# Attention products with V: which are issued in halves, and behind which group of scores

## The chip, the cores and the metric

The kernel runs on one core of a Trainium2 chip. The metric is the time of one execution on the device, in microseconds (us). A core has five engines that this text speaks of: PE (TensorE, matrix products; its weight loads are shown apart as PEld), DVE (VectorE), ACT (ScalarE), POOL (GpSimd) and SP (SyncE, which here only issues transfers). Each works through its own instructions in order and waits for the others by semaphores.

## The reference

Two attention blocks over 2048 tokens with 512 channels and 32 heads of 16 are mixed by a gate. A attends causally inside segments of 512 tokens and adds a compressive memory; B attends over all 2048 tokens.

```python
g = _sigmoid((x * gate_w).sum(-1, keepdims=True))
# A, for each of four segments s:
logits = einsum("bhqd,bhkd->bhqk", qs, ks) * scale + mask      # 512 x 512, causal
a_dot = einsum("bhqk,bhkd->bhqd", softmax(logits), vs)
o = gm * num / den + (1 - gm) * a_dot                          # gm = sigmoid(beta); num, den from M, z
M = M + einsum("bhld,bhle->bhde", phi(ks), vs)
# B:
p = softmax(einsum("bhqd,bhkd->bhqk", q, k) * Dh ** -0.5)      # 2048 x 2048
out = g * (concat(o) @ A_wo) + (1 - g) * (einsum("bhqk,bhkd->bhqd", p, v) @ B_wo)
```

## The kernel before

**Units and slots.** A unit is four heads by 512 queries. There are 32 units of A and 32 of B, and after a first phase (projections, the memory, all keys and values to DRAM and back) the kernel runs 32 slots; slot k computes unit k of A and unit 32+k of B. A unit of B has 16 blocks of 128 keys, one of A has four blocks of its own segment, of which the causal mask leaves 512, 384, 256 and 128 query columns.

**Groups.** A slot is a loop over 37 groups (`NG`). Groups 0 to 31 belong to B: group n takes block n//2 and one pair of its four heads. Groups 32 to 36 belong to A (`GA`, packed so that each fills two banks of 512 columns: block 0 in groups 32 and 33, blocks 1 and 3 together in 34 and 35, block 2 in 36). In each group, in this order:

- `t_group` writes the transposed scores of two heads to two banks of PSUM (L502, two matmuls, side by side on halves of the array) and has ACT turn each bank into exponentials in the buffer `raw` (L508). Three banks are used in turn (`T3`: two `tb` and `mb`), so the second bank of a group is the first bank of the group before, and is free only when ACT has read it. For A, POOL then zeroes the masked corner of what ACT wrote (L511).
- The tasks of `plan`: as a rule one piece of the plain scores of a later unit, `s_b` (L448) or in groups 32 to 36 and 0 `s_a` (L427, L430), whose maximum DVE takes (L450, L434, L436). These go to two double banks, `sbk`.
- In group 20 of the slots from 9 on, one half of an output projection, `out_mm` (L590, twelve matmuls into one of the three banks); its result is copied by ACT (even halves, L594) or added by DVE (odd halves, L597).
- `pvs(k, n)`: products of the exponentials with V, by `pv` (L524). For each of the four heads a matmul of 17 columns of weights (16 of V and one of ones, which gives the softmax's sum) accumulates in a strip of 32 partitions of one bank, `pvb`; the trace shows two records for each such matmul.

**The products before.** For B, block b's product is issued in two halves of 256 query columns, the first in group 2b+2 and the second in group 2b+3; so each group from 2 to 33 holds one half, and block 15 falls into groups 32 and 33, beside A's first scores. After the second half of block 15 `fin_copy` (L533, ACT) takes the bank `pvb` to `pvs` and stores it. Then follow A's products into the same bank: block 0 in two halves in groups 34 and 35, blocks 1 and 3 in group 36, block 2 in group 0 of the next slot, with its `fin_copy` (L531, DVE). Group 1 has no product. Slot 31 issues B's blocks whole, in odd groups, and has two banks more for its scores.

Behind group 21 of a slot stands `m_chain` (L459 to L469, four small operations of DVE on the maxima), and its result is spread into the queries by `m_rows` in group 24. `fin_load`, `fin_rec`, `fin_bc` and `fin_norm` carry the stored sums and outputs of a unit through division and gate; they lie beside the groups on SP, DVE and POOL.

Of the kernel before, what the change touches and what calls it, by code (L numbers as in the profile page):

```python
# [23 lines left out]
NT = SEQ // 128  # L24
# [5 lines left out]
OMI = 10  # L30
# [3 lines left out]
def gated_mix_kernel(ctx, tc, x, wq, wk, wv, wo, beta, wqkv, wob, gate_w, out):  # L34
# [479 lines left out]
    def pv(u, it, lo=0, hi=None):  # L514

        kd, qd, c = UN[u]
        g, q = divmod(qd, 2)
        q0 = 128 * it if kd == "A" else 0
        hi = hi or C - q0
        last = 2 if kd == "A" else NT - 1  # L520
        vt = VA[(u // 2) % 2] if kd == "A" else VB[g % 2]
        for h in range(4):
            pt = PT[u, it, h]
            nc.tensor.matmul(PVB[32 * h:32 * h + E + 1, q0 + lo:q0 + hi], vt[:, it, 4 * q + h, :], pt[:, lo:hi],  # L524
                             start=it == 0 and lo == 0, stop=it == last and q0 + hi == C, skip_group_check=True)

    def fin_copy(u):

        ps = W.tile([128, C], FT, name="pvs", bufs=1)
        if u < 31:  # L530
            nc.vector.tensor_copy(ps, PVB)  # L531
        else:
            nc.scalar.activation(ps, PVB, AF.Copy)  # L533
        AT["pd", u] = D.tile([4, 32, C], FT, name=f"pd{u}")
        nc.sync.dma_start(AT["pd", u].rearrange("h r t -> (h r) t"), ps)
# [36 lines left out]
    def load_wo(g):  # L572
        for a, w in enumerate((wo, wob)):
            raw = AT["o"][1][:, g, a]
            nc.sync.dma_start(raw, w[g * 128:(g + 1) * 128, :])
            nc.gpsimd.tensor_copy(AT["wh"][:, g, a], raw)
            nc.gpsimd.tensor_tensor(AT["wl"][:, g, a], raw, AT["wh"][:, g, a], op=OP.subtract)
# [142 lines left out]
    for blk in range(16):  # L720
# [12 lines left out]
        n = blk + 1 + (c == 2)  # L733
# [92 lines left out]
    def pvs(k, n):  # L826

        ua, ub = k, 32 + k
        if n == 0:
            if k:  # L830
                pv(ua - 1, 2)
                fin_copy(ua - 1)
        elif k == 31 and n < 2 * NT:
            if n % 2 and n > 1:
                pv(ub, n // 2 - 1)
        elif 2 <= n < 2 * NT + 2:
            pv(ub, n // 2 - 1, n % 2 * 256, n % 2 * 256 + 256)
            if n == 2 * NT + 1:
                fin_copy(ub)
        elif n > 2 * NT + 1:  # L840
            m = n - 2 * NT - 2
            if m < 2:
                pv(ua, 0, 256 * m, 256 * m + 256)
            else:
                pv(ua, 1)
                pv(ua, 3)

    def extras(k):

# [55 lines left out]
    for k in range(32):  # L905
        ua, ub = k, 32 + k
        banks = T3 + [SBK[0][:, n] for n in range(2)] * (k == 31)
        for n in range(NG):
            it = n // 2 if n < NG - 1 else NT + 2
            t_group(*(ub, n) if n < 2 * NT else (ua, n - 2 * NT), banks)  # L910
            for f in plan.get((k, n), []) + ex[k][0].get(n, []):
                f()
            pvs(k, n)
            for f in ex[k][1].get(n, []):
                f()
# [19 lines left out]
            if it == 9:  # L935
                if k % 2 == 0 and k < 30:
                    load_vb(k // 2 + 1)
                if 1 <= k <= 4:
                    load_wo(k - 1)
    pv(31, 2)  # L940
    fin_copy(31)
    fin_bc(63)
    den = AT["d"][0][64:]
# [51 lines left out]
```

## Time and profile before

| what | value |
|---|---|
| three timed runs | 2005.86, 2013.76, 2010.57 us (median 2010.57) |
| the profiled execution's own time | 2007.75 us |
| its span in the profile | 2006.0 us, granted clock 0.995 |
| one slot, 1 to 8 (between the DVE copies L531) | 47.96 to 48.71 us |
| one slot, 9 to 29 | 50.89 to 52.54 us |
| DVE, ACT, POOL busy, share of the span | 81%, 72%, 13% |

A row of the timeline gives the start and the length in us, engine, line, operation, what it writes and reads, the shapes, how many instructions are merged in it, and in brackets how long the engine was idle before and what ended that. A row of waits gives the engine and line that waited, for whom, the total in us, how often, and the longest. A PE record contains the filling and emptying of the array, so two records in a row overlap; how long a matmul holds PE is read from start to start.

### The profile page before, as it was taken

The numbers are of one execution on the slowest core, as the hardware profiler recorded it, in microseconds if no ns is written. First come the engines' busy times: TensorE is split into PE (matmuls) and PEld (weight loads), VectorE is DVE, ScalarE is ACT, GpSimd is POOL, SyncE is SP. The second block draws the span as 40 slices with busy tenths as digits, with TensorE's granted clock in tenths as the row PEclk, the third lists the DMA queues.
The fourth block names the chain that finished last, engine by engine and source line by source line (L and its number), as shares of the span: only waits on it lengthen the run. The fifth ranks groups of instructions, "written<-read, shape, count | busy, mean of one in ns | idle before, by whom it ended". The sixth has DMA issues, their size and how long they took to land.

```text
span 2006.0 us, 43688 instructions
## 1 busy us (share of the span) xinstructions
PE 1956.3 (98%) x17517; PEld 949.0 (47%) x17517; DVE 1631.9 (81%) x1825; ACT 1435.1 (72%) x2703; POOL 256.6 (13%) x474
## 2 busy tenths in 40 slices
PE   8999999999999999999999999999999999999988
PEld 7777777444444344444444444444444444444434
DVE  6135665799999999999999999999899999899832
ACT  3233332688888888888787888787878787878883
POOL 2200000011110101111111111111111111111111
PEclk9999999999999999999999999999999999999999
DMA  7765656644443445343435344444444545444101
GB/s 222 164 190 177 197 180 177 148 106 112 95 112 85 104 93 109 81 110 81 109 79 112 85 112 85 112 85 112 85 112 85 112 85 111 85 112 85 50 26 54
DMA packets 162743, 222.49 MB, mean 111 GB/s; under 512 B 39261, under 2 KB 89453, under 8 KB 156781
## 3 DMA queue, kind: packets, MB, share of 16 engines
q1 hardware_dynamic: 159596, 211.70, 43.9%
q0 software_dynamic: 2944, 8.00, 2.2%
q8 instruction: 138, 2.26, 0.5%
q14 instruction: 65, 0.52, 0.1%
HBM read 148.21 MB, written 68.16 MB: 108 GB/s over the span
## 4 chain that ended last, share of the span: by engine, by line
PE 89%; DMA 3%; DVE 3%; ACT 2%; SPq 2%; issue 1%; POOL 0%; ACTq 0%; POOLq 0%; DVEq 0%
PE pvb L524 31%; PE tb L502 17%; PE sbk L448 12%; PE mb L502 8%; PE tb L279 3%; PE sbk L427 2%; PE tb L590 2%; PE mb L279 2%; ACT raw L508 2%; PE pvb L279 2%; DVE mxb L450 2%; PE sbk L430 2%; PE mb L590 1%; PE sbk L279 1%; PE tb L262 1%
## 5 line engine op out<-in xcount | busy, mean ns | idle before, releaser
L450 DVE TENSOR_REDUCE mxb<-sbk 128x2 f32<-128x1024 f32 x1024 | 1222.7, 1222 | 49.4 <-PE sbk L448 45.7
L508 ACT ACTIVATE raw<-tb 128x512 f32<-128x512 f32 x1557 | 886.0, 596 | 172.8 <-PE tb L502 85.6
L524 PE MATMUL pvb<-raw,vb 128*17 128x256 f32 (+1 forms) x8072 | 639.5, 389 | 0.0
L508 ACT ACTIVATE raw<-mb 128x512 f32<-128x512 f32 x780 | 465.2, 596 | 81.6 <-PE tb L502 57.5
L502 PE MATMUL tb<-qb,xh 64*128 64x512 f32 x880 | 330.9, 494 | 3.7 <-ACT raw L508 3.7
L524 PEld LDWEIGHTS pvb<-raw,vb 128*17 128x17 f32 x8072 | 133.8, 95 | 344.8 <-issue 338.4
L448 PE MATMUL sbk<-xh,qb 64*128 64x512 f32 x1344 | 287.6, 400 | 4.4 <-DVE mxb L450 3.3
L511 POOL TENSOR_SCALAR_AFFINE_SELECT raw<-raw 128x256 f32<-128x256 f32 (+1 forms) x320 | 115.4, 361 | 879.9 <-ACT raw L508 871.9
L502 PE MATMUL mb<-qb,xh 64*128 64x512 f32 x437 | 215.6, 493 | 2.0 <-ACT raw L508 2.0
L502 PEld LDWEIGHTS tb<-qb,xh 64*128 64x128 f32 x880 | 124.7, 183 | 190.5 <-issue 98.3
L502 PE MATMUL tb<-qb,kb 64*128 64x512 f32 x463 | 176.0, 496 | 4.8 <-ACT raw L508 2.8
L434 DVE TENSOR_REDUCE mx<-sbk 128x2 f32<-128x768 f32 (+1 forms) x128 | 139.8, 1092 | 43.9 <-PE sbk L430 36.2
L448 PE MATMUL sbk<-kb,qb 64*128 64x512 f32 x704 | 152.9, 408 | 0.8 <-DVE mxb L450 0.7
L448 PEld LDWEIGHTS sbk<-xh,qb 64*128 64x128 f32 x1344 | 138.8, 186 | 10.8 <-DVE mxb L450 7.0
L502 PEld LDWEIGHTS mb<-qb,xh 64*128 64x128 f32 x437 | 79.9, 183 | 89.5 <-issue 49.1
L502 PE MATMUL mb<-qb,kb 64*128 64x512 f32 x241 | 118.4, 491 | 0.8 <-DVE st L289 0.8
L502 PEld LDWEIGHTS tb<-qb,kb 64*128 64x128 f32 x463 | 65.8, 183 | 102.3 <-issue 51.4
L524 PE MATMUL pvb<-raw,va 128*17 128x256 f32 (+2 forms) x1280 | 94.7, 383 | 4.2 <-ACT pvs L533 0.8
L564 POOL TENSOR_TENSOR o<-o,d 128x512 f32<-128x512 f32 x31 | 39.7, 1282 | 415.2 <-DMA qa<-dA 177.0
L427 PE MATMUL sbk<-ka,qa 64*128 64x256 f32 (+3 forms) x512 | 86.6, 346 | 0.0
L502 PE MATMUL tb<-qa,ka 64*128 64x384 f32 (+3 forms) x340 | 79.5, 372 | 0.0
L448 PEld LDWEIGHTS sbk<-kb,qb 64*128 64x128 f32 x704 | 72.1, 185 | 12.6 <-issue 6.5
(265 smaller groups left out, 1804.5 us busy)
## 6 DMA issues: line engine op xcount, KB each, us to landing
xh<-dB SPq DMA_DIRECT2D x38, 512.0 KB
vb<-vdB SPq DMA_DIRECT2D x16, 1088.0 KB
dB<-st SPq DMA_DIRECT2D x64, 256.0 KB
dA<-st SPq DMA_DIRECT2D x64, 256.0 KB
pd<-pvs SPq DMA_DIRECT2D x64, 256.0 KB
kb<-dB SPq DMA_DIRECT2D x22, 512.0 KB
xh<-dB SPq DMA_DIRECT2D x38, 256.0 KB
qb<-dB SPq DMA_DIRECT2D x64, 128.0 KB
```

The source lines that it names most:

```text
L279: nc.tensor.matmul(b, WS[ws][w][wi][:, k, :], (XH, XL)[xi][c][:, k, :], start=n == 0, stop=n == 11)
L427: nc.tensor.matmul(b[:, j, c0:c0 + n], q_of(u)[r, p, i * 128:(i + 1) * 128], k_of(u, p)[r, :n], start=True, stop=False)
L430: nc.tensor.matmul(b[:, j, c0 + n - 128:c0 + n], crows[r, n2 - 1], cmask[r, n2 - 1], start=False, stop=n2 == 2)
L434: nc.vector.tensor_reduce(m[:, :, p, i], b[:, :, :n], axis=AX.X, op=OP.max)
L448: nc.tensor.matmul(b[:, j], q_of(u)[r, p, i * 128:(i + 1) * 128], k_of(u, p)[r, kc * C:(kc + 1) * C], start=True, stop=True)
L450: nc.vector.tensor_reduce(MXB[u][:, :, p, i, kc], b, axis=AX.X, op=OP.max)
L502: nc.tensor.matmul(bs[j][:, c0:c0 + w], k_of(u, h // 2)[r, 128 * it:128 * it + 128], q_of(u)[r, h // 2, q0:], start=True, stop=True)
L508: nc.scalar.activation(pt, bs[j], AF.Exp, scale=SCALE)
L511: nc.gpsimd.affine_select(out=m, in_=m, pattern=[[1, 128]] if n < 2 else [[0, 2], [1, 128]], compare_op=OP.is_ge, fill=0.0, base=0, channe ...
L524: nc.tensor.matmul(PVB[32 * h:32 * h + E + 1, q0 + lo:q0 + hi], vt[:, it, 4 * q + h, :], pt[:, lo:hi], start=it == 0 and lo == 0, stop=it ...
L564: nc.gpsimd.tensor_tensor(o, o, d, op=OP.mult)
L590: nc.tensor.matmul(b, (AT["oh"], AT["ol"])[oi][:, g, a], (AT["wh"], AT["wl"])[wi][:, g, a], start=n == 0, stop=n == 11)
```

## The change

Only the table of products in `pvs` and its remainder behind the loop change.

- B's block 15 is issued whole (512 columns) in group 32, and `fin_copy` of B's unit follows there; group 33 has no product.
- A's block 0 is issued whole in group 34; group 35 and group 36 have no product.
- A's blocks 1 and 3 move from group 36 to group 0 of the next slot, ahead of block 2, whose place stays. Behind the last slot the three follow the loop.
- In slots 9 to 30, B's block 9 is issued whole in group 20, behind `out_mm`; group 21 has no product.
- All other products of B stay as they were.

```diff
         if n == 0:
             if k:
-                pv(ua - 1, 2)
+                for it in (1, 3, 2):
+                    pv(ua - 1, it)
                 fin_copy(ua - 1)
-        elif k == 31 and n < 2 * NT:
+        elif n == 2 * NT:
+            pv(ub, NT - 1)
+            fin_copy(ub)
+        elif n > 2 * NT:
+            if n == 2 * NT + 2:
+                pv(ua, 0)
+        elif k == 31:
             if n % 2 and n > 1:
                 pv(ub, n // 2 - 1)
-        elif 2 <= n < 2 * NT + 2:
+        elif k >= 9 and n // 2 == OMI:
+            if n % 2 == 0:
+                pv(ub, n // 2 - 1)
+        elif n > 1:
             pv(ub, n // 2 - 1, n % 2 * 256, n % 2 * 256 + 256)
-            if n == 2 * NT + 1:
-                fin_copy(ub)
-        elif n > 2 * NT + 1:
-            m = n - 2 * NT - 2
-            if m < 2:
-                pv(ua, 0, 256 * m, 256 * m + 256)
-            else:
-                pv(ua, 1)
-                pv(ua, 3)
...
-    pv(31, 2)
+    for it in (1, 3, 2):
+        pv(31, it)
     fin_copy(31)
```

PE at the end of a slot's B part (here slot 0), groups 32 and 33: `vb` is B's V, `qa` and `ka` are A's queries and keys, and the L502 rows are the transposed scores of groups 33 and 34.

```order
 L430 MATMUL sbk_113<-cmask,crows 128x128
-L524 MATMUL pvb<-raw_86,vb_75 17x256 x4
+L524 MATMUL pvb<-raw_86,vb_75 17x512 x4
 L502 MATMUL mb<-qa_73,ka_71 128x512
 L502 MATMUL tb_109<-qa_73,ka_71 128x512
@@ -608,5 +608,4 @@
 L430 LDWEIGHTS crows
 L430 MATMUL sbk_114<-cmask,crows 128x128
-L524 MATMUL pvb<-raw_86,vb_75 17x256 x4
 L502 MATMUL tb_110<-qa_73,ka_71 128x384
 L502 MATMUL mb<-qa_73,ka_71 128x384
```

Both halves now stand ahead of group 33's scores, and group 34's scores follow group 33's with only the plain scores and their mask between them.

ACT at the same place: L508 are the exponentials of groups 32 and 33, L533 is the copy of B's finished bank.

```order
 L508 ACTIVATE raw_86<-tb_109 128x512
 L508 ACTIVATE raw_86<-tb_110 128x512
-L508 ACTIVATE raw_86<-mb 128x512
-L508 ACTIVATE raw_86<-tb_109 128x512
-L533 ACTIVATE pvs<-pvb 128x512
+L533 ACTIVATE pvs<-pvb 128x512
+L508 ACTIVATE raw_86<-mb 128x512
+L508 ACTIVATE raw_86<-tb_109 128x512
```

The copy now stands ahead of group 33's two exponentials, which wait behind it for the end of the whole product.

PE behind the projection of slot 9, before: L590 is the projection's end, L524 are B's products, L502 the scores of groups 21 and 22, L448 plain scores.

```order
L590 MATMUL tb_110<-wh,ol 128x512 x4
L524 MATMUL pvb<-raw_86,vb_75 17x256 x4
L502 MATMUL mb<-qb_70,kb_89 128x512
L502 MATMUL tb_109<-qb_70,kb_89 128x512
L448 MATMUL sbk_114<-xh_88,qb_69 128x512 x2
L524 MATMUL pvb<-raw_86,vb_75 17x256 x4
L502 MATMUL tb_110<-qb_70,kb_89 128x512
```

The same place in the changed kernel:

```order
L590 MATMUL tb_110<-wh,ol 128x512 x4
L524 MATMUL pvb<-raw_86,vb_75 17x512 x4
L502 MATMUL mb<-qb_70,kb_89 128x512
L502 MATMUL tb_109<-qb_70,kb_89 128x512
L448 MATMUL sbk_114<-xh_88,qb_69 128x512 x2
L502 MATMUL tb_110<-qb_70,kb_89 128x512
L502 MATMUL mb<-qb_70,kb_89 128x512
```

The first product has 512 columns and the second is gone, so the scores of group 22 stand right behind the plain scores of group 21.

## The prediction

> **What bounds the kernel now.** I began with the page's head and its busy shares.
>
> ```profile
> span 2006.0 us, 43688 instructions
> PE 1956.3 (98%) x17517; PEld 949.0 (47%) x17517; DVE 1631.9 (81%) x1825; ACT 1435.1 (72%) x2703; POOL 256.6 (13%) x474
> ```
>
> PE looks full, so whatever shortens PE's work should help. But an overlapping record hides a wait between two matmuls, so I read the one kind of group that already has no product, group 1 of a slot (here of slot 20), on the timeline.
>
> ```profile
> 1364.09 0.49 PE L502 MATMUL mb<-qb,xh 64*128 64x512 f32 x1
> 1364.09 0.49 PE L502 MATMUL tb<-qb,xh 64*128 64x512 f32 x1
> 1364.42 0.40 PE L448 MATMUL sbk<-kb,qb 64*128 64x512 f32 x2
> ...
> 1364.65 0.39 PE L502 MATMUL tb<-qb,xh 64*128 64x512 f32 x1
> 1364.68 0.60 ACT L508 ACTIVATE raw<-mb 128x512 f32<-128x512 f32 x1 [0.38 <-PE tb L502]
> ...
> 1365.33 0.49 PE L502 MATMUL mb<-qb,xh 64*128 64x512 f32 x1 [0.29 <-ACT raw L508]
> ...
> 1365.99 0.63 PE L524 MATMUL pvb<-raw,vb 128*17 128x256 f32 x8
> ...
> 1366.54 0.50 PE L502 MATMUL tb<-qb,xh 64*128 64x512 f32 x2
> ```
>
> Group 1's scores start at 1364.09, and PE is through its plain scores 0.56 us later: the first matmul of group 2 starts at 1364.65. The second needs the bank `mb` that ACT is reading, whose exponential ends at 1365.28, and starts at 1365.33. So **a group without a product takes 1.24 us**, and the next, with half a product, takes 1365.33 to 1366.54 = 1.21 us. The product fits into the time that a bank needs to go round: 0.53 to 0.59 from a score's start to its exponential's, 0.60 for that, 0.03 to 0.05 to the next matmul, together 1.16 to 1.24. PE's own time with half a product is about the same, so in an ordinary group both bind at once, and a half taken out of a group frees nothing.
>
> DVE is no bound in between:
>
> ```profile
> 1343.45 3.48 DVE L450 TENSOR_REDUCE mxb<-sbk 128x2 f32<-128x1024 f32 x3
> ```
>
> Back to back, three maxima take 3.48, so they start every (3.48 - 1.22) / 2 = 1.13 us, against 1.21 to 1.24 of a group.
>
> **What a product costs PE.** Half a product and the projection's surroundings (slot 19):
>
> ```profile
> 1339.32 1.07 PE L590 MATMUL mb<-wh,ol 128*128 128x512 f32 x4
> 1340.32 0.63 PE L524 MATMUL pvb<-raw,vb 128*17 128x256 f32 x8
> ...
> 1340.87 0.50 PE L502 MATMUL tb<-qb,xh 64*128 64x512 f32 x2
> 1341.21 0.40 PE L448 MATMUL sbk<-kb,qb 64*128 64x512 f32 x2
> 1341.40 1.09 ACT L508 ACTIVATE raw<-tb 128x512 f32<-128x512 f32 x2 [0.39 <-PE tb L502]
> 1341.54 0.63 PE L524 MATMUL pvb<-raw,vb 128*17 128x256 f32 x8
> ...
> 1342.10 0.49 PE L502 MATMUL tb<-qb,xh 64*128 64x512 f32 x1
> ```
>
> A whole one, in slot 31:
>
> ```profile
> 1965.76 1.05 PE L524 MATMUL pvb<-raw,vb 128*17 128x512 f32 x8
> ...
> 1966.74 0.50 PE L502 MATMUL tb<-qb,xh 64*128 64x512 f32 x2
> ```
>
> From start to start a half holds PE 1340.87 - 1340.32 = 0.55 us and a whole 0.98: a merge costs its first group 0.43 and saves 2 x 0.55 - 0.98 = 0.12 of PE in sum. The saving can only be had if the group that lost its half gets shorter by 0.55.
>
> **Edit 1: block 9 whole behind the projection** (slots 9 to 30, 22 of them). PE goes straight from L590 to the product; ACT and DVE have run dry. Group 21's scores start at 1340.87 + 0.43 = 1341.30. Before, group 22's second matmul came 1342.10 - 1340.87 = 1.23 later. Now PE could be there after 0.34 + 0.33 = 0.67 (the steps to L448 and to L524 above), but the bank is busy: group 21's exponential starts 0.53 after its scores (1341.40), takes 0.60 and releases 0.03 to 0.05 later, 1.16 to 1.18. So group 22 is late by 0.43 - 0.06 = **0.37**; bounds 0.30 (the half could gain as much as 0.13) and 0.44 (the 1.24 of group 1). Later groups carry a half again and cannot make it up. Sum 22 x 0.37 = 8.1, between 6.6 and 9.7.
>
> **Edit 2: the end of a slot** (31 places, from slot 0's group 32 to slot 30's, with group 0 of the next). Slot 19:
>
> ```profile
> 1354.76 0.49 PE L502 MATMUL mb<-qa,ka 64*128 64x512 f32 x1
> ...
> 1355.65 0.63 PE L524 MATMUL pvb<-raw,vb 128*17 128x256 f32 x8
> ...
> 1356.20 0.49 PE L502 MATMUL tb<-qa,ka 64*128 64x512 f32 x1
> ...
> 1356.79 0.60 ACT L508 ACTIVATE raw<-tb 128x512 f32<-128x512 f32 x1 [0.42 <-PE mb L502]
> 1356.99 0.62 PE L524 MATMUL pvb<-raw,vb 128*17 128x256 f32 x8
> ...
> 1357.55 0.50 PE L502 MATMUL tb<-qa,ka 64*128 64x384 f32 x4
> 1357.76 0.60 ACT L533 ACTIVATE pvs<-pvb 128x512 f32<-128x512 f32 x1
> ...
> 1358.01 0.29 POOL L511 TENSOR_SCALAR_AFFINE_SELECT raw<-raw 128x128 f32<-128x128 f32 x1 [0.20 <-ACT raw L508]
> ...
> 1358.48 0.16 PEld L524 LDWEIGHTS pvb<-raw,va 128*17 128x17 f32 x8 [0.26 <-POOL raw L511]
> ...
> 1359.07 0.44 PE L502 MATMUL tb<-qa,ka 64*128 64x384 f32 x1
> ...
> 1359.67 0.60 ACT L508 ACTIVATE raw<-mb 128x512 f32<-128x512 f32 x1 [0.32 <-PE tb L502]
> 1359.86 0.63 PE L524 MATMUL pvb<-raw,va 128*17 128x256 f32 x8
> ...
> 1360.42 0.38 PE L502 MATMUL tb<-qa,ka 64*128 64x256 f32 x1
> ...
> 1361.69 1.06 PE L524 MATMUL pvb<-raw,va 128*17 128x384 f32 x16
> ...
> 1362.68 0.49 PE L502 MATMUL tb<-qb,xh 64*128 64x512 f32 x2
> ...
> 1363.53 0.63 PE L524 MATMUL pvb<-raw,va 128*17 128x256 f32 x8
> ```
>
> From group 32 to group 1 of the next slot it takes 1364.09 - 1354.76 = 9.33 us: 1.44, 1.35, 1.52, 1.35, 2.26 and 1.41. Then:
> - *Group 32* has the whole: 1.44 + 0.43 = 1.87.
> - *Group 33* has none. PE alone would need 0.79 (1356.20 to 1356.99). But ACT now has L533 ahead of its exponentials, and L533 waits for the whole product: its start 1355.65, its record 1.05 and 0.1 to ACT give 1356.80; one ACT operation later (0.48) the exponential starts at 1357.28 instead of the 1357.15 that its scores, now at 1356.63, would allow. With 0.60 and 0.03 group 34's second matmul starts at 1357.91: 1.28 for the group.
> - *Group 34* has A's block 0 whole, which needs POOL's select on group 33's second exponential; POOL's last started 1358.01 and PE 0.47 later. The exponential comes 0.49 behind the first, so now at 1357.77, which is 0.48 later than before (0.50 behind the 1356.79 above), and the product at 1358.48 + 0.48 = 1358.96. With 0.98 the next scores start at 1359.94, so 2.03.
> - *Group 35* has none. PE alone: 0.79. The bank: 0.60 to the exponential (1359.07 to 1359.67), 0.60 and 0.03: 1.23.
> - *Group 36* has none: 1361.69 - 1360.42 = 1.27 of scores and plain scores, after which group 0 follows at once; its bank is free after 1.23 and does not hold it.
> - *Group 0*: 0.85 to the product (1362.68 to 1363.53), then the two moved ones, 1362.68 - 1361.69 = 0.99, and block 2's 0.56: 2.40. POOL has long finished.
>
> Sum 1.87 + 1.28 + 2.03 + 1.23 + 1.27 + 2.40 = 10.08, **0.75** more. The bounds: if neither L533 nor POOL costs anything (1.16 and 0.79 + 0.98 = 1.77 for groups 33 and 34, 1.16 and 1.20 for 35 and 36) it is 9.56, or +0.23; if groups 33, 35 and 36 gain nothing at all (1.35, 1.35 and 1.36) it is 10.36, or +1.03. I take the value by the rows. Sum 31 x 0.75 = 23.3, between 7.1 and 31.9.
>
> Queued behind the added waits: L531 waits on DVE for the later end of block 2, and the maxima behind it start at about group 1's plain scores anyway; the stores of `pvs` leave SP about 0.7 later and are read many groups on. The moved operations issue no other transfers.
>
> **The tail.** Slot 31 has two more banks and whole products already; there block 15's copy comes earlier, A's products later. One row for the first:
>
> ```profile
> 1971.93 0.60 ACT L533 ACTIVATE pvs<-pvb 128x512 f32<-128x512 f32 x1
> ```
>
> By the rule of group 32 it starts some 0.9 earlier, and PE's last products some 0.6 later; I count 0, within 1 us either way.
>
> **Sum.** 2007.75 + 8.1 + 23.3 = 2039.2 us on the profiled execution's own time, which is 2.8 under the median shown; so **2039**. Bounds 2007.75 + 13.7 = 2021 and 2007.75 + 41.6 = 2049.
>
> **Rivals.**
>
> *PE's work decides (faster).* Block 15 and block 0 in 32 slots and block 9 in 22 are 86 merges at 0.12, or 10.3 us less: 1997. It holds if a group without product ends with PE's own 0.67 to 0.79, that is if the bank's round were shorter than that. For it: 98% busy. The Trainium skill (Perfetto Trace Analysis, Engine Utilization) says that in a well-optimized kernel at least one engine should approach full utilization, which read for PE gives this rival. Against it: 0.29 of idle ahead of L502 in a group that has no product. The Trainium skill (TensorE: Matmul & The Clock Gate, Wait — 56ns, not 53.3ns?) puts the fixed cost of one more back-to-back matmul at about 2.5 ns; eight records fewer in a merge would be 0.02 us, an estimate from that page, and this rival would then be worth 1.7 us; the rows above show 0.12, and they decide. 0.07.
>
> *The end of the slot comes out even.* Before, ACT stands still behind group 36 while blocks 1 and 3 run:
>
> ```profile
> 1363.21 1.09 ACT L508 ACTIVATE raw<-tb 128x512 f32<-128x512 f32 x2 [1.11 <-PE tb L502]
> ```
>
> The change starts these exponentials earlier. Were 0.75 of the 0.99 hidden under them, edit 1 alone would remain: 2016. Against it: group 0 holds only 1.1 of ACT's work and would be 2.40 long, so ACT stands still there instead. 0.08.
>
> *DVE collides.* Group 24's plain scores wait for the maximum behind `m_chain`.
>
> ```profile
> PE sbk L448 <- DVE mxb L450: 3.9, 6, 1.3
> ```
>
> Edit 1 shifts that maximum 0.43 and the scores only 0.37, so such waits can become more; at 1.3 in each of the eleven even slots from 10 to 30 they would add 14: 2053. 0.07.
>
> **How the numbers follow.** The forecast has 0.78. Its own range is 2021 to 2049; with the spread of the runs (5 below to 3 above their median) and part of the third rival I give **2020 to 2052**. A measurement of this kernel can tell about 0.5%, 10 us, from no change. Faster by more: the first rival, 0.07. Within: the second, 0.08, and little else. Slower: 0.85.
>
> **What would show it.** Right: in groups 33, 35 and 21, PE's rows L502 idle before ACT's L508, as only group 1 shows it now; groups 32 to 1 add up to about 10.1; slots 1 to 8 take 48.7, the later ones 52.0; DVE's and ACT's busy time is unchanged. Wrong: if group 33 or 21 is shorter than 1.1, the bank does not bind and the first rival holds; if group 0 to 1 is well under 2.4, the moved products are hidden; if the loss is there but L448 waits for DVE, it is the third.

## The result and the profile after

The changed kernel takes 2058.53 us (median of 6 runs, 2056.88 to 2065.93) against 2008.07 before (median of 6): a ratio of 1.0252, with a 95% interval of 1.023 to 1.0273. It is slower, as forecast, but by 50 us instead of 31, and outside the range.

The page's head of the changed kernel:

```profile
span 2059.8 us, 42280 instructions
PE 1971.4 (96%) x16829; PEld 961.3 (47%) x16829; DVE 1635.3 (79%) x1825; ACT 1432.7 (70%) x2703; POOL 256.4 (12%) x474
```

The busy times of ACT, DVE and POOL are as before: the 50 us are waiting. PE's row shows that only in part: its busy time grew by 15 us, although its products take less of it.

From start to start of DVE's copy L531, a slot of 1 to 8 took 47.99 us before (median) and 49.34 now, an odd slot from 9 on 50.92 and 52.69. So a slot's end costs 1.35, and the projection's group another 0.4. 31 x 1.35 + 22 x 0.4 = 51, about the whole difference. (An even slot from 10 on grew by less, from 51.18 to 52.64, and in the two profiled executions the 30 slots between the first L531 and the last differ by 46.9. The profiled execution itself took 2061.52, 3 over the median; its first slot began about 5 us later than that of before, in a part in which the two programs are alike.)

Who waited on PE in the changed kernel (in us: total, times, longest), the first three rows:

```profile
PE sbk L427 <- DVE mx L436: 22.1, 30, 0.7
PE tb L502 <- ACT raw L508: 18.4, 76, 0.4
PE mb L502 <- ACT raw L508: 9.0, 38, 0.5
```

The second and third are the forecast waits for a bank of transposed scores; the same two rows before had 6.5 and 2.0 us. The first is new, and the prediction doesn't have it: `s_a` of group 0 (L427) waits until DVE has read the double bank that it writes (L436).

The end of slot 19 on the timeline, the rows that answer to those shown of before:

```profile
1389.44 0.49 PE L502 MATMUL mb<-qa,ka 64*128 64x512 f32 x1
...
1390.33 1.05 PE L524 MATMUL pvb<-raw,vb 128*17 128x512 f32 x8
...
1391.32 0.49 PE L502 MATMUL tb<-qa,ka 64*128 64x512 f32 x1
...
1391.48 0.60 ACT L533 ACTIVATE pvs<-pvb 128x512 f32<-128x512 f32 x1 [0.42 <-PE pvb L524]
...
1392.62 0.44 PE L502 MATMUL tb<-qa,ka 64*128 64x384 f32 x2 [0.22 <-ACT raw L508]
...
1393.40 1.17 PE L524 MATMUL pvb<-raw,va 128*17 128x512 f32 x8
...
1394.49 0.44 PE L502 MATMUL mb<-qa,ka 64*128 64x384 f32 x1
...
1395.74 0.38 PE L502 MATMUL mb<-qa,ka 64*128 64x256 f32 x1 [0.22 <-ACT raw L508]
...
1396.80 0.58 PE L502 MATMUL tb<-qb,xh 64*128 64x512 f32 x2
1396.83 1.23 DVE L436 TENSOR_REDUCE mx<-sbk 128x4 f32<-128x1024 f32 x1 [0.47 <-PE sbk L430]
...
1398.11 0.33 PE L427 MATMUL sbk<-ka,qa 64*128 64x128 f32 x2 [0.74 <-DVE mx L436]
...
1398.74 1.49 PE L524 MATMUL pvb<-raw,va 128*17 128x384 f32 x24
...
1400.16 0.49 PE L502 MATMUL mb<-qb,xh 64*128 64x512 f32 x1
```

| group | before | forecast | after |
|---|---|---|---|
| 32 (block 15 whole) | 1.44 | 1.87 | 1.88 |
| 33 (none) | 1.35 | 1.28 | 1.30 |
| 34 (block 0 whole) | 1.52 | 2.03 | 1.87 |
| 35 (none) | 1.35 | 1.23 | 1.25 |
| 36 (none) | 2.26 | 1.27 | 1.06 |
| 0 (blocks 1, 3 and 2) | 1.41 | 2.40 | 3.36 |
| sum | 9.33 | 10.08 | 10.72 |

Groups 32, 33 and 35 came out as worked out, groups 34 and 36 shorter. Group 0 is 0.96 too long, and the rows say why: its scores start at 1396.80, the plain scores L427 only 1.31 later instead of 0.33, when the maximum L436 ends (1396.83 + 1.23 = 1398.06).

### The profile page after: what moved, and what is told of

Same layout as the page of the kernel before. It is cut to its first block, busy times and chain, and to the rows that moved or that the text cites. A ratio compares the mean times of both kernels' runs of the same rounds, so it can differ in the third digit from the quotient of the medians.

```text
span 2059.8 us, 42280 instructions
## 1 busy us (share of the span) xinstructions
PE 1971.4 (96%) x16829; PEld 961.3 (47%) x16829; DVE 1635.3 (79%) x1825; ACT 1432.7 (70%) x2703; POOL 256.4 (12%) x474
## 4 chain that ended last, share of the span: by engine, by line
PE 81%; ACT 6%; DMA 4%; DVE 3%; issue 3%; POOL 2%; SPq 1%; ACTq 0%; POOLq 0%; DVEq 0%
PE pvb L524 29%; PE tb L502 16%; PE sbk L448 11%; PE mb L502 7%; ACT raw L508 4%; PE tb L279 3%; PE tb L590 2%; PE mb L279 2%; PE sbk L427 2%; DVE mxb L450 1%; PE mb L590 1%; PE pvb L279 1%; DVE mx L436 1%; PE sbk L430 1%; POOL ol L584 1%
## 5 line engine op out<-in xcount | busy, mean ns | idle before, releaser
L450 DVE TENSOR_REDUCE mxb<-sbk 128x2 f32<-128x1024 f32 x1024 | 1226.1, 1221 | 59.4 <-PE sbk L448 56.4
L508 ACT ACTIVATE raw<-tb 128x512 f32<-128x512 f32 x1557 | 883.7, 596 | 208.8 <-PE tb L502 118.1
L524 PE MATMUL pvb<-raw,vb 128*17 128x256 f32 (+1 forms) x7640 | 628.7, 401 | 0.0
L508 ACT ACTIVATE raw<-mb 128x512 f32<-128x512 f32 x780 | 464.8, 596 | 86.1 <-PE tb L502 54.1
L502 PE MATMUL tb<-qb,xh 64*128 64x512 f32 x880 | 333.7, 491 | 6.8 <-ACT raw L508 6.8
L448 PE MATMUL sbk<-xh,qb 64*128 64x512 f32 x1344 | 294.4, 401 | 4.6 <-DMA xh<-dB 2.4
L524 PEld LDWEIGHTS pvb<-raw,vb 128*17 128x17 f32 x7640 | 126.7, 95 | 332.9 <-issue 329.5
L502 PEld LDWEIGHTS tb<-qb,xh 64*128 64x128 f32 x880 | 127.7, 183 | 202.2 <-ACT raw L508 98.6
L502 PE MATMUL mb<-qb,xh 64*128 64x512 f32 x437 | 213.8, 489 | 2.0 <-ACT raw L508 2.0
L502 PE MATMUL tb<-qb,kb 64*128 64x512 f32 x463 | 173.8, 492 | 4.7 <-ACT raw L508 2.8
L448 PE MATMUL sbk<-kb,qb 64*128 64x512 f32 x704 | 156.4, 408 | 0.0
L448 PEld LDWEIGHTS sbk<-xh,qb 64*128 64x128 f32 x1344 | 142.5, 186 | 10.9 <-DVE mxb L450 5.2
L502 PE MATMUL mb<-qb,kb 64*128 64x512 f32 x241 | 118.0, 490 | 2.8 <-ACT raw L508 2.0
L502 PEld LDWEIGHTS mb<-qb,xh 64*128 64x128 f32 x437 | 79.9, 183 | 85.9 <-issue 45.9
L427 PE MATMUL sbk<-ka,qa 64*128 64x256 f32 (+3 forms) x512 | 98.4, 357 | 22.1 <-DVE mx L436 22.1
L502 PEld LDWEIGHTS tb<-qb,kb 64*128 64x128 f32 x463 | 65.7, 183 | 97.1 <-issue 47.6
L502 PE MATMUL tb<-qa,ka 64*128 64x384 f32 (+3 forms) x340 | 90.7, 381 | 8.8 <-ACT raw L508 8.8
L524 PE MATMUL pvb<-raw,va 128*17 128x512 f32 (+3 forms) x1024 | 86.5, 435 | 0.3 <-POOL raw L511 0.2
L430 PE MATMUL sbk<-cmask,crows 64*128 64x128 bf16 x1024 | 83.5, 221 | 0.0
```

The lines of the kernel that those rows point to most:

```text
L427: nc.tensor.matmul(b[:, j, c0:c0 + n], q_of(u)[r, p, i * 128:(i + 1) * 128], k_of(u, p)[r, :n], start=True, stop=False)
L430: nc.tensor.matmul(b[:, j, c0 + n - 128:c0 + n], crows[r, n2 - 1], cmask[r, n2 - 1], start=False, stop=n2 == 2)
L448: nc.tensor.matmul(b[:, j], q_of(u)[r, p, i * 128:(i + 1) * 128], k_of(u, p)[r, kc * C:(kc + 1) * C], start=True, stop=True)
L450: nc.vector.tensor_reduce(MXB[u][:, :, p, i, kc], b, axis=AX.X, op=OP.max)
L502: nc.tensor.matmul(bs[j][:, c0:c0 + w], k_of(u, h // 2)[r, 128 * it:128 * it + 128], q_of(u)[r, h // 2, q0:], start=True, stop=True)
L508: nc.scalar.activation(pt, bs[j], AF.Exp, scale=SCALE)
```

## The experiments

Theory S: a slot's end lost 1.35 through two things, the bank's round as forecast and the wait for the double bank, which blocks 1 and 3 had covered while they stood between group 36's plain scores and group 0's. Its rival R: all of it comes from the whole products and the copy L533 in groups 32 to 34.

**Block 9 alone.** Before, with

```diff
+        elif k >= 9 and n // 2 == OMI:
+            if n % 2 == 0:
+                pv(ub, n // 2 - 1)
         elif 2 <= n < 2 * NT + 2:
```

> Of the change only B's block 9 whole in group 20 of slots 9 to 30. Theory (a group without a product still takes the 1.16 to 1.24 us of a bank's round, and group 20 pays 0.43): slots 9 to 29 grow by 0.37 to 0.43, in all 8 to 9 us more than before. Rival (PE's work decides): 22 x 0.12 = 2.6 us less than before.

Measured: 1.0035 of before (1.002 to 1.005), about 7 us more. Slots 1 to 8 stay at 48.03, odd ones from 9 on go from 50.92 to 51.33, even ones from 10 on from 51.18 to 51.36. Slot 19 in this kernel, PE and ACT behind the projection:

```profile
1348.45 1.05 PE L524 MATMUL pvb<-raw,vb 128*17 128x512 f32 x8
...
1349.43 0.50 PE L502 MATMUL tb<-qb,xh 64*128 64x512 f32 x2
...
1349.96 1.09 ACT L508 ACTIVATE raw<-tb 128x512 f32<-128x512 f32 x2 [0.81 <-PE tb L502]
1350.00 0.39 PE L502 MATMUL mb<-qb,xh 64*128 64x512 f32 x1
...
1350.61 0.49 PE L502 MATMUL tb<-qb,xh 64*128 64x512 f32 x1 [0.23 <-ACT raw L508]
```

The whole holds PE 0.98, group 21 takes 1350.61 - 1349.43 = 1.18 without a product, and PE idles until ACT releases the bank, as edit 1 of the prediction has it.

**The move alone.** Before, with blocks 1 and 3 taken from group 36 to group 0:

```diff
-                pv(ua - 1, 2)
+                for it in (1, 3, 2):
+                    pv(ua - 1, it)
                 fin_copy(ua - 1)
...
-            else:
-                pv(ua, 1)
-                pv(ua, 3)
...
-    pv(31, 2)
+    for it in (1, 3, 2):
+        pv(31, it)
```

> Of the change only A's blocks 1 and 3 moved from group 36 to group 0, all halves as before. Theory S (in group 0 the plain scores of A's block 0, s_a, wait for their double bank, whose maximum L436 was covered by the 0.99 of blocks 1 and 3 before): from group 36 to group 1 it takes 4.4 to 4.6 us instead of 3.67, PE idles about 0.7 ahead of L427 in group 0, in all 23 to 30 us more than before. Rival R (the extra loss comes from whole products and the copy L533 in groups 32 to 34): 3.67 as before, nothing in sum.

Measured: 1.0111 (1.0082 to 1.0139), about 22 us more; slots 1 to 8 take 48.75. The first row of who waited on PE, and the place in slot 19:

```profile
PE sbk L427 <- DVE mx L436: 19.1, 30, 0.6
```

```profile
1380.10 1.23 DVE L436 TENSOR_REDUCE mx<-sbk 128x4 f32<-128x1024 f32 x1 [0.57 <-PE sbk L430]
1380.18 0.58 PE L502 MATMUL tb<-qb,xh 64*128 64x512 f32 x2
...
1381.38 0.33 PE L427 MATMUL sbk<-ka,qa 64*128 64x128 f32 x2 [0.63 <-DVE mx L436]
```

The wait is there with every product in halves, so it belongs to the move. Group 36 and group 0 together take 1383.43 - 1379.01 = 4.42 here, against 3.67 before. R falls for this part: it had nothing here.

**The whole products alone.** Before, with block 15 and its copy in group 32 and block 0 in group 34:

```diff
+        elif n == 2 * NT:
+            pv(ub, NT - 1)
+            fin_copy(ub)
+        elif n > 2 * NT:
+            if n == 2 * NT + 2:
+                pv(ua, 0)
+            elif n == 2 * NT + 4:
+                pv(ua, 1)
+                pv(ua, 3)
...
-            if n == 2 * NT + 1:
-                fin_copy(ub)
-        elif n > 2 * NT + 1:
-            m = n - 2 * NT - 2
-            if m < 2:
-                pv(ua, 0, 256 * m, 256 * m + 256)
-            else:
-                pv(ua, 1)
-                pv(ua, 3)
```

> Of the change only B's block 15 and A's block 0 whole (groups 32 and 34), blocks 1 and 3 left in group 36, block 9 in halves. Theory S: groups 32 to 36 take 1.88 + 1.30 + 1.87 + 1.25 = 6.30 us instead of 5.66, and group 36 on is as before: 31 x 0.64 = 20 us more than before. Rival R: the whole 1.33 of a slot's end comes from here, 41 us more.

Measured: 1.0087 (1.0057 to 1.0116), about 17 us more; slots 1 to 8 take 48.61, or 0.62 more, against 0.64 expected, and R's 41 us are not there. The three parts alone add up to 7 + 22 + 17 = 46 of the 50.

**The changed kernel with group 0 in another order.**

```diff
+            if n == 0:
+                pvs(k, n)
             for f in plan.get((k, n), []) + ex[k][0].get(n, []):
                 f()
-            pvs(k, n)
+            if n:
+                pvs(k, n)
```

> The changed kernel with one thing swapped: in group 0 of a slot the three products of A stand ahead of the plain scores s_a instead of behind them. Theory S: the wait of L427 for L436 (22.1 us in 30 times in the changed kernel, 0.96 from the start of L502 to L427 beyond the usual 0.33) goes, group 0 takes 2.4 instead of 3.36, in all about 30 us less than the changed kernel, about 2029. Rival R: nothing changes, 2058.

Measured: 2028.19 us, 1.0094 of before (1.0069 to 1.0118): 30 us less than the changed kernel, as expected. The same place of slot 19 in this kernel:

```profile
1373.94 0.58 PE L502 MATMUL tb<-qb,xh 64*128 64x512 f32 x2
1373.97 1.23 DVE L436 TENSOR_REDUCE mx<-sbk 128x4 f32<-128x1024 f32 x1 [0.47 <-PE sbk L430]
...
1374.45 1.49 PE L524 MATMUL pvb<-raw,va 128*17 128x384 f32 x24
...
1375.87 0.33 PE L427 MATMUL sbk<-ka,qa 64*128 64x128 f32 x2
1376.03 0.29 PE L430 MATMUL sbk<-cmask,crows 64*128 64x128 bf16 x4
...
1376.38 0.47 PE L502 MATMUL tb<-qb,xh 64*128 64x512 f32 x1
```

The products cover the maximum again, L427 waits for nobody, and group 0 takes 1376.38 - 1373.94 = 2.44, close to the 2.40 that the prediction had counted.

**The move alone, in that order.**

The edits of the two experiments above together, on the kernel before.

> The move of A's blocks 1 and 3 alone (as in e2_move_only), with the three products of group 0 ahead of its s_a. Theory S: the wait of L427 for L436 (19.1 us in 30 times in e2_move_only) goes, and group 36 and group 0 take 1.27 + 2.40 = 3.67 as before: slots 1 to 8 about 48.0, no difference from before that can be told. Rival (the move costs by itself, through ACT standing still in group 0): slots 1 to 8 stay at 48.75, 22 us more than before.

Measured: 1.0001 (0.9985 to 1.0016), slots 1 to 8 at 47.94. The list of waits no longer has a row of L427 waiting for L436. Moving two products behind the next scores costs and brings nothing that can be told from the spread of the runs; what cost was that the plain scores stood ahead of them.

**Two halves left out.** Before, without the second halves of blocks 5 and 12:

```diff
+        elif n in (13, 27):
+            pass
         elif 2 <= n < 2 * NT + 2:
```

> Of before, with work left out: in slots 0 to 30 the second halves of B's blocks 5 and 12 (groups 13 and 27) aren't computed, 62 halves of 0.55 us of PE. Theory (a bank's round): groups 13 and 27 get shorter by 0.06 at most, 0 to 4 us in all, and PE idles in front of the next group's L502 until ACT's L508. Rival (PE's work decides, DVE has 0.09 a group to spare and two buffers): up to 62 x 0.55 = 34 us less.

Measured: 0.9984 of before (0.9972 to 0.9996), 3 us less; slots 1 to 8 take 48.00, as with the halves. 62 x 0.55 = 34 us of PE's work are gone. A group 13:

```profile
1378.02 0.50 PE L502 MATMUL tb<-qb,xh 64*128 64x512 f32 x1
1378.35 0.39 PE L448 MATMUL sbk<-kb,qb 64*128 64x512 f32 x2
1378.59 0.38 PE L502 MATMUL tb<-qb,xh 64*128 64x512 f32 x1
1378.61 0.60 ACT L508 ACTIVATE raw<-mb 128x512 f32<-128x512 f32 x1 [0.22 <-PE mb L502]
1379.10 1.08 ACT L508 ACTIVATE raw<-tb 128x512 f32<-128x512 f32 x2
1379.26 0.49 PE L502 MATMUL mb<-qb,xh 64*128 64x512 f32 x1 [0.29 <-ACT raw L508]
```

It takes 1379.26 - 1378.02 = 1.24, ended by ACT. Less work for PE alone makes such a group no shorter.

**Can the room of group 1 be used?** Two tries on the kernel before. The first moves block 3 and the copy of A's bank:

```diff
-        last = 2 if kd == "A" else NT - 1
+        last = 3 if kd == "A" else NT - 1
...
                 pv(ua - 1, 2)
-                fin_copy(ua - 1)
...
                 pv(ua, 1)
-                pv(ua, 3)
...
+            if n == 1 and k:
+                pv(ua - 1, 3)
+                fin_copy(ua - 1)
             for f in plan.get((k, n), []) + ex[k][0].get(n, []):
...
     pv(31, 2)
+    pv(31, 3)
```

> Of before, with one other move: A's block 3 (128 columns, 0.33 us of PE) goes from group 36 to group 1 of the next slot, right behind its scores and ahead of its plain scores, with the DVE copy of A's bank. Theory (group 1 has room, since the bank's round makes it 1.24 long with 0.56 to 0.66 of PE's work): group 36 becomes 0.33 shorter, group 1 stays at 1.24, s_a of group 0 gives back at most 0.06 of it by its wait for L436; 31 x 0.27 = 8 us less than before, up to 10. Rival (PE's work decides): the work is only moved, nothing changes.

Measured: 1.002 (1.0007 to 1.0033), 4 us more: a miss. Slot 19's next groups 0 to 4, PE and then DVE:

```profile
1364.82 0.50 PE L502 MATMUL tb<-qb,xh 64*128 64x512 f32 x2
...
1366.34 0.50 PE L502 MATMUL tb<-qb,xh 64*128 64x512 f32 x1
1366.77 0.41 PE L524 MATMUL pvb<-raw,va 128*17 128x128 f32 x8
...
1367.58 0.50 PE L502 MATMUL mb<-qb,xh 64*128 64x512 f32 x1
...
1368.80 0.49 PE L502 MATMUL tb<-qb,xh 64*128 64x512 f32 x2
1369.18 0.49 PE L448 MATMUL sbk<-kb,qb 64*128 64x512 f32 x2
...
1370.17 0.50 PE L502 MATMUL mb<-qb,xh 64*128 64x512 f32 x1
```

```profile
1367.30 0.69 DVE L531 COPY pvs<-pvb 128x512 f32<-128x512 f32 x1 [0.48 <-issue]
1367.91 3.48 DVE L450 TENSOR_REDUCE mxb<-sbk 128x2 f32<-128x1024 f32 x3
```

Group 1 carries the product and still takes 1367.58 - 1366.34 = 1.24; that was right. But the copy now stands ahead of group 1's maximum, which starts at 1367.91, 1.57 behind the group's scores. Group 3's plain scores need its double bank (1367.91 + 1.22 = 1369.13, then 1369.18), and the group takes 1.37 instead of 1.22. Group 0 takes 1.52 instead of 1.41. Together they return what group 36 saved.

The second moves `s_a` of block 0 to group 1:

```diff
-            plan.setdefault((k, 2 * NT + n) if n < 5 else (k + 1, 0), []).append(todo(s_a, k + 1, *t))
+            plan.setdefault((k, 2 * NT + n) if n < 5 else (k + 1, 1), []).append(todo(s_a, k + 1, *t))
```

> Of before, with one other move: s_a of A's block 0 (0.52 us of PE with its mask) goes from group 0 to group 1, ahead of that group's s_b; all products stay as before. Theory (group 1 has room under the bank's round, group 0 then needs only its own round of 1.16 to 1.24 instead of 1.41): slots become 0.1 to 0.25 us shorter, after up to 0.1 for the double bank in group 2; 3 to 7 us less than before. Rival (PE's work decides, it is only moved): nothing changes. Also possible, as with block 3 in group 1: DVE's order takes it back, and nothing changes with PE waiting for DVE ahead of L448.

Measured: 1.0000 (0.9986 to 1.0014). The possibility named last came true: in this kernel the list of waits has

```profile
PE sbk L448 <- DVE mx L436: 5.3, 30, 0.2
```

which before hadn't. In slot 19 group 0 takes 0.98 instead of 1.41 and group 2 1.65 instead of 1.21: its plain scores (L448) start only when L436 has ended. Neither try beat the kernel before.

## Why the prediction was right and where it failed

**What bounds an ordinary group: right.** Without a product, groups 13, 21, 33 and 35 took 1.18 to 1.30 us, and taking 34 us of products out of ordinary groups brought 3. The first rival, PE's work, falls with it. The Trainium skill (Perfetto Trace Analysis, Engine Utilization) looks for one engine near full utilization in a well-optimized kernel. PE was near it at 98%, and still the time hardly moved with its work, so here the row of busy shares didn't show what holds such a group: the round of a bank.

**Edit 1: right.** 0.37 expected a slot, 0.41 measured alone in odd slots; in even slots from 10 on it was 0.18, and in all the edit cost about 7 us (4 to 10) against 8.1 forecast.

**Edit 2, groups 32 to 35: near in sum, with one wait misread.** 6.41 forecast, 6.30 measured. Group 33 went as told: the copy L533 stands ahead of its exponentials, and the group takes 1.30 against 1.28. (The 0.02, there and in group 35, are the release of a bank: the sum counted 0.03, and the prediction's own row of group 1 shows 0.05, from 1365.28 to 1365.33.) Group 34 was 0.16 cheaper, and the prediction's reading of it was wrong. It took the time from POOL's last select to the product, 0.47, for the price of that wait. Before, the product also had to wait for L533, which reads the bank `pvb` that the product writes:

```profile
1357.76 0.60 ACT L533 ACTIVATE pvs<-pvb 128x512 f32<-128x512 f32 x1
1358.01 0.29 POOL L511 TENSOR_SCALAR_AFFINE_SELECT raw<-raw 128x128 f32<-128x128 f32 x1 [0.20 <-ACT raw L508]
...
1358.51 0.63 PE L524 MATMUL pvb<-raw,va 128*17 128x256 f32 x8
```

The select ended at 1358.30 and the copy at 1358.36. In all 32 slots of before the product starts 0.14 to 0.15 behind the copy's end, while its distance from the select's end goes from 0.21 to 0.28. In the changed kernel the copy has ended at 1392.08, long before, and the product starts at 1393.40, while POOL's last select still runs (1393.18 to 1393.47). So it starts 0.27 earlier in its group than forecast, and it holds PE 0.11 longer.

**Edit 2, groups 36 and 0: the step that failed** is "*Group 0*: 0.85 to the product (1362.68 to 1363.53)". It was read at a place of the kernel before where L427's double bank had just come free:

```profile
1361.52 1.23 DVE L436 TENSOR_REDUCE mx<-sbk 128x4 f32<-128x1024 f32 x1 [0.58 <-PE sbk L430]
...
1363.01 0.22 PE L427 MATMUL sbk<-ka,qa 64*128 64x128 f32 x2
```

The maximum ended at 1362.75 and L427 started 0.26 later. The prediction took the 0.99 of blocks 1 and 3 away from between the two and didn't ask what they had covered there; it followed `raw` and the banks of transposed scores through the move, but not `sbk`. Group 0 takes 3.36 instead of 2.40 and group 36 0.21 less, so 0.75 a slot are missing; groups 32 to 35 return 0.11, and 31 x 0.64 = 20 us are about what the sum lacked (50 - 31 = 19). Group 36's 1.27 was a second, smaller slip: it was read up to the start of a product, and where scores follow instead it is 1.17 (1379.01 to 1380.18 in the move alone). The rest of the 0.21 wasn't tested; in the changed kernel one of group 36's scores starts at 1395.16, ahead of the wait for the bank that ends at 1395.74. In front of the wait for `sbk` a shorter group 36 gains nothing. That this wait is the cause was tested from both sides: the order of group 0 alone takes 30 us off the changed kernel, and the move in that order costs nothing. Groups 36 and 0 together, 3.67 before and in the forecast, take 4.42 in the changed kernel and in the move alone, and 3.50 and 3.60 where the products come first.

**The rivals.** The second, a slot's end that comes out even, fell too. The move alone in the other order did come out even, but not because products were hidden under ACT's exponentials: ACT stands still 1.50 there behind the products of group 0, where before it stood still 1.11 behind those of group 36. The third, DVE's collision in group 24, didn't come: the row of L448 waiting for L450 fell from 3.9 us to 1.8. The range was too narrow because every case in it kept the 0.85, and none of the signs that the prediction named for being wrong was this wait.

## What to carry to other kernels

When work is moved, ask of both its neighbours what it covered: list each buffer that the instruction behind it writes, and who must have emptied it. An engine that is 98% busy by its records may still be held by a buffer's round; a group that already lacks the work in question shows it without an experiment. And room found on one engine isn't room in the kernel, as both tries with group 1 show: the order on DVE took it back.

## What was not expected of the hardware

A product of four heads doesn't wait as one. In the changed kernel the whole product of A's block 0 starts 0.07 before POOL's last select ends (1393.40 against 1393.47), is 1.17 us long in its row instead of 1.05, and holds PE 1394.49 - 1393.40 = 1.09 instead of 0.98. Two windows of the trace, for L524 on PE alone, count its records (x):

```profile
1393.30:1393.50 0.20, 0.10 (x3) 1.00 0.97 379
1393.30:1393.60 0.30, 0.20 (x4) 1.00 1.03 382
```

Three heads start before the select ends; the fourth, whose corner that select zeroes, starts at 1393.53, 0.05 behind the select's end. The rows read so that each head waits for its own select; the 0.13 between the third head and the fourth accounts for the 0.11 that the product holds PE longer.
